# Linear attention and a squared-ReLU layer on one core: whole-group q loads, more dummy matmuls, a 384/128 last tile, and another instruction order

## The chip, the cores and the metric

The kernel runs on one core of one Trainium2 chip. A core has five engines that each run their own list of instructions in order: TensorE (PE in the profile, with its weight loads as PEld), VectorE (DVE), ScalarE (ACT), GpSimd (POOL) and SyncE (SP). Here POOL and SP mostly issue DMA transfers. The metric is the device time of one execution in microseconds (us).

## The reference

Inputs are q, k, v of shape (8 batches, 8 heads, 576 tokens, 64), a feature matrix w_phi (64 x 128), and the weights w_in (512 x 2048) and w_out (2048 x 512) of a two-layer network.

```
phi(x):  proj = x @ w_phi
         proj = proj - max(|proj|)            # per token and head
         return concat(exp(proj), exp(-proj)) # 256 features
kv  = sum over tokens of phi(k)^T v           # per batch and head
z   = sum over tokens of phi(k)
x   = (phi(q) @ kv) / (phi(q) @ z + 1e-6)     # heads side by side: 4608 x 512
out = relu(x @ w_in)^2 @ w_out                # 4608 x 512, float32
```

## The kernel before

**Tiling.** Each batch has 576 tokens: 512 "main" ones and 64 at the end. A main tile holds 128 partitions with four tokens each. The output layer takes tokens in chunks of 512: chunks 0 to 7 are the main tokens of batches 0 to 7, chunk 8 gathers the last 64 tokens of all eight batches (buffer `xS`).

**Attention of one batch** (`attention(b)`). k, q and v are loaded by POOL with a cast to bf16 into `xk`, `xq`, `xv`, two buffers each, so batch b+2 reuses the buffer of batch b. k and q must then be transposed so that the head dimension lies on partitions (`kT`, `qT`). For batches 0 and 1 PE does it with an identity (L307) and ACT or DVE copies the result; from batch 2 on SP issues a DMA transpose of the whole tile (L317). PE multiplies by `wphi2` (L333 and L482 give token-major projections whose absolute maximum DVE takes, L388 and L489; L524 gives feature-major projections of q), ACT takes the exponentials into `kp`, `kn`, `qp`, `qn` (L394, L539). PE sums `kv` (L449, L454), and later multiplies q features with it (L603, once with `qp`, once with `qn`, DVE scaling in between, L615). DVE divides (L625, L629) into `xo`, and from batch 1 on SP issues another DMA transpose from `xo` into `xT` (L663).

**The two layers.** `ffn_in` (L744, for chunk 0 in smaller pieces at L755, L769, L783) fills one bank of PSUM with 512 columns; ACT or DVE takes the ReLU into `hr` (L721, L723) and DVE squares it into `h2` (L730). `ffn_out` (L837) sums 16 matmuls of 512 columns per output tile, ACT or DVE copies the bank into `ot` (three buffers in a ring; the copy is line L190 on DVE and L192 on ACT), and SP issues the store (L855, and L852 for chunk 8). The very last output tile goes through `last_out` (L801): two halves of 256 columns in two banks, ACT copying the first and DVE the second into `otl`, then four stores (L824), two from SP and two from ACT.

**Order.** Nothing is left to a scheduler. Each step is an `Op` with an engine and a place in the list of its creation (`seq`). `ORDER` lists all of them in the order in which they are issued, and every engine executes its own part of that list in sequence. `BASES` gives each PSUM tile its bank, `STATES` chooses between ACT and DVE for copies and ReLUs that either can do (`plan.either`), and `GATES` names, for loads from batch 2 on, an earlier step after which the load may go out. `FILL` names steps before which dummy matmuls of a zero tile `warm` are put on PE (L910), as (bank, count). The waits themselves follow from the data.

```
for op in plan.arrange():
    if op.seq in FILL:
        now[0] = filler
        bank, n = FILL[op.seq]
        for _ in range(n):
            pin(nc.tensor.matmul(out=psum[:, bank, :P], lhsT=warm, rhs=warm, start=True, stop=True))
    now[0] = op
    op.fn()
```

**Layout of q.** `load_q` splits the four tokens of a partition into two pairs (`jj`) and puts, for each pair, the eight heads side by side: block t = 8 * jj + h of 128 columns. From batch 2 on it does so in `PIECES`, one pair of heads per transfer: eight transfers per batch, each with runs of 128 numbers.

Of the kernel before, what the change touches and what calls it, by code (L numbers as in the profile page):

```python
# [107 lines left out]
def kernel(  # L108
# [150 lines left out]
    def load_q(b, jjs=(0, 1), single=True, release=False, prs=((0, 4),)):  # L259

        x = xq[b % 2]
        for jj in jjs:
            for a, z in prs:
                def fn(jj=jj, a=a, z=z):
                    pin(nc.gpsimd.dma_start(  # L265
                        out=x[:, jj * 1024 + a * 256 : jj * 1024 + z * 256].rearrange("p (h x) -> p h x", x=128),
                        in_=q[b][2 * a : 2 * z, 0:512, :].rearrange("h (p j) d -> p h (j d)", j=4)[:, :, jj * 128 : jj * 128 + 128]))
                add("POOL", (0.72, 0), fn, w=([("xq", b % 2, jj)] if z == 4 else []) + [("xq", b % 2, jj, y) for y in range(a, min(z, 3))],
                     dma=(work(b, LD["main"] / 8 * (z - a)), SW_IN, "ld", late(b)), release=release, what="xq")
        if single:  # L270
            load(q, xq, b, "xq", prs=(), release=release)
# [23 lines left out]
    def attention(b):  # L295
# [173 lines left out]
        def q_ts(c):  # L469
            if c == 4:  # L470
                return [16, 17]
            return [8 * (c // 2) + h for h in range(8)] if first else [8 * (c // 2) + 4 * (c % 2) + i for i in range(4)]
# [36 lines left out]
        def q_ops(c):  # L509
# [3 lines left out]
            def fn():  # L513
                o = ps2(pf)
                for u in range(2):
# [5 lines left out]
                    else:  # L521
                        r = slice(64 * u, 64 * u + 64)
                        rhs = qTb[r, ts[0] : ts[-1] + 1, :]
# [269 lines left out]
    def last_out(c, tt, part):  # L793
# [3 lines left out]
        gs = opb[c, tt]  # L797
        def mm(half):
            def fn():
                for mc in range(4 * part, 4 * part + 4):  # L800
                    pin(nc.tensor.matmul(out=ps1(gs[half])[:, :256], lhsT=h2[c % 2][mc // 4][:, mc % 4, tt * P : (tt + 1) * P],  # L801
                                         rhs=wout[mc // 4][:, mc % 4, half * 256 : half * 256 + 256],
                                         start=(mc == 0), stop=(mc == MC - 1)))
            return fn
        for half in range(2):
            add("PE", pe_cost(4, 0.109), mm(half),
# [4 lines left out]
        for half in range(2):  # L811
            def fn(half=half):
                o, i_ = otl[:, half * 256 : half * 256 + 256], ps1(gs[half])[:, :256]
# [4 lines left out]
            add("DVE" if half else "ACT", (dve_cost if half else act_cost)(256), fn, r=[gs[half]],  # L818
                w=[("otl", half)], closes=gs[half], what="oth")
        for half in range(2):  # L820
            for u, (name, e) in enumerate((("SP", nc.sync), ("ACT", nc.scalar))):
                def fn(half=half, u=u, e=e):
                    b = 2 * tt + u
                    pin(e.dma_start(out=out[b * S + 512 : b * S + 576, half * 256 : half * 256 + 256],  # L824
                                    in_=otl[u * 64 : u * 64 + 64, half * 256 : half * 256 + 256]))
                add(name, (0.5, 2.4), fn, r=[("otl", half)], what="stl")
# [237 lines left out]
```

## Time and profile before

| | us |
|---|---|
| median of three runs | 357.9 (357.79 to 360.02) |
| the profiled execution | 359.46 |
| its span, first to last instruction | 357.7 |
| TensorE busy | 343.7 (96%) |
| VectorE busy | 276.4 (77%) |
| ScalarE busy | 227.9 (64%) |
| GpSimd busy (issue of loads) | 113.1 (32%) |

"Busy" is the time in which an engine had an instruction in work; on TensorE it includes the dummy matmuls. The profile also has a table of the span in 40 slices of 8.9 us, groups of instructions by source line, the chain of waits, and lists in order of time in which "[2.02 <-DMA out]" means that the engine sat idle for 2.02 us before the instruction and what ended it. SPq and POOLq are issues of transfers; "landed" is the time at which a transfer's last byte was reported.

### The profile page before, as it was taken

How to read it: one execution, taken by the hardware profiler on the slowest of the kernel's cores; microseconds unless marked ns; L12 is line 12 of the kernel's file. 1: busy time of each engine (PE TensorE's matmuls, PEld its weight loads, DVE VectorE, ACT ScalarE, POOL GpSimd, SP SyncE). 2: the span in 40 equal slices, each digit the busy share in tenths (PEclk: the TensorE clock that was granted, in tenths of full speed). 3: DMA queues.
4: the chain of work that ended last, by engine and by line, in shares of the span. 5: the costliest groups of instructions: out<-in, count | busy, mean ns of one | idle time of the engine just before them, and what ended most of it. 6: DMA issues, size and time to landing. Idle time of an engine off the chain costs nothing.

```text
span 357.7 us, 8393 instructions
## 1 busy us (share of the span) xinstructions
PE 343.7 (96%) x3344; PEld 194.8 (54%) x3374; DVE 276.4 (77%) x523; ACT 227.9 (64%) x429; POOL 113.1 (32%) x168
## 2 busy tenths in 40 slices
PE   6999999799999999999999999999999999999995
PEld 4789667444566455446545545455546554444443
DVE  3899899969979998799868899998849762673621
ACT  3999898549886876776689766786684700312211
POOL 8723764395706940594806000003000000000000
PEclk9999999989999999999999999999999999999999
DMA  9999999999988999796999574405400312000124
GB/s 99 187 205 199 95 165 135 162 182 171 115 130 175 141 131 177 162 158 85 127 183 148 98 98 76 139 9 58 95 3 31 95 39 88 2 0 0 73 77 117
DMA packets 102647, 39.61 MB, mean 111 GB/s; under 512 B 77264, under 2 KB 98128, under 8 KB 102608
## 3 DMA queue, kind: packets, MB, share of 16 engines
q0 software_dynamic: 51760, 18.36, 47.7%
q1 hardware_dynamic: 50608, 20.55, 27.2%
q8 instruction: 26, 0.43, 0.5%
q10 hardware_dynamic: 240, 0.16, 0.2%
q14 instruction: 13, 0.11, 0.1%
HBM read 36.77 MB, written 9.44 MB: 129 GB/s over the span
## 4 chain that ended last, share of the span: by engine, by line
PE 73%; ACT 8%; DVE 7%; POOL 4%; DMA 3%; issue 3%; SPq 0%; POOLq 0%; ACTq 0%; DVEq 0%
PE psum L837 29%; PE psum L744 24%; PE psum L603 5%; PE psum L333 4%; DVE va L421 3%; PE psum L449 2%; PE psum L524 2%; DMA xv<-in_v_dram 2%; POOL xk L245 2%; ACT qp L539 2%; ACT qn L539 1%; DMA out_dram<-ot 1%; DVE mq L489 1%; DVE h L730 1%; PE psum L769 1%
## 5 line engine op out<-in xcount | busy, mean ns | idle before, releaser
L837 PE MATMUL psum<-wout,h 128*128 128x512 bf16 x530 | 130.2, 381 | 2.3 <-issue 1.0
L744 PE MATMUL psum<-xT,win 128*128 128x512 bf16 x448 | 104.7, 380 | 0.5 <-ACT hr L721 0.3
L721 ACT ACTIVATE hr<-psum 128x512 bf16<-128x512 f32 x95 | 55.4, 599 | 61.8 <-PE psum L744 45.7
L837 PEld LDWEIGHTS <-h 128*128 128x128 bf16 x560 | 50.8, 98 | 54.3 <-issue 1.7
L744 PEld LDWEIGHTS <-win 128*128 128x128 bf16 x512 | 47.4, 98 | 53.8 <-issue 2.7
L730 DVE TENSOR_TENSOR h<-hr 128x512 bf16<-128x512 bf16 x144 | 56.0, 417 | 9.6 <-ACT hr L721 8.9
L539 ACT ACTIVATE qp<-psum 128x1024 bf16<-128x1024 f32 (+1 forms) x40 | 37.4, 936 | 18.1 <-PE psum L524 14.9
L489 DVE TENSOR_REDUCE mq<-psum 128x8 f32<-128x1024 f32 (+1 forms) x40 | 43.8, 1111 | 6.0 <-PE psum L333 5.3
L265 POOL DMA_DIRECT2D xq<-in_q_dram x52 | 39.1, 778 | 23.1 <-ACT va L413 17.4
L723 DVE TENSOR_SCALAR hr<-psum 128x512 bf16<-128x512 f32 x49 | 33.3, 685 | 14.8 <-PE psum L744 14.1
L388 DVE TENSOR_REDUCE mk<-psum 128x8 f32<-128x1024 f32 (+1 forms) x35 | 38.3, 1109 | 3.9 <-PE psum L333 3.5
L394 ACT ACTIVATE kp<-psum 128x1024 bf16<-128x1024 f32 (+1 forms) x35 | 32.8, 937 | 12.1 <-DVE mk L388 12.0
L245 POOL DMA_DIRECT2D xv<-in_v_dram x27 | 20.5, 767 | 59.6 <-DVE kv L190 49.1
L539 ACT ACTIVATE qn<-psum 128x1024 bf16<-128x1024 f32 (+1 forms) x40 | 37.4, 936 | 1.6 <-PE psum L603 1.6
L394 ACT ACTIVATE kn<-psum 128x1024 bf16<-128x1024 f32 (+1 forms) x35 | 32.7, 938 | 0.0
L615 DVE TENSOR_TENSOR psum<-psum,en 128x520 f32<-128x520 f32 (+1 forms) x39 | 26.9, 701 | 6.9 <-PE psum L603 4.8
L421 DVE TENSOR_TENSOR va<-xv,va 64x256 bf16<-64x256 bf16 (+2 forms) x66 | 29.8, 473 | 2.6 <-ACT va L413 1.6
L629 DVE TENSOR_TENSOR xo<-psum,rden 128x512 bf16<-128x512 f32 (+1 forms) x39 | 26.8, 687 | 0.9
L190 DVE COPY ot<-psum 128x512 f32<-128x512 f32 x19 | 12.9, 681 | 18.4 <-PE psum L837 15.2
L245 POOL DMA_DIRECT2D xk<-in_k_dram x28 | 21.2, 766 | 10.7 <-ACT qp L539 6.6
L449 PE MATMUL psum<-va,kp 128*128 128x65 bf16 x256 | 19.8, 193 | 0.3 <-ACT hr L721 0.3
L192 ACT ACTIVATE ot<-psum 128x512 f32<-128x512 f32 x16 | 9.6, 598 | 15.8 <-PE psum L837 13.8
(81 smaller groups left out, 408.6 us busy)
## 6 DMA issues: line engine op xcount, KB each, us to landing
out_dram<-ot SPq DMA_DIRECT2D x32, 256.0 KB, 2.8
xk<-in_k_dram POOLq DMA_DIRECT2D x26, 128.0 KB, 4.1
xq<-in_q_dram POOLq DMA_DIRECT2D x48, 64.0 KB, 4.3
xv<-in_v_dram POOLq DMA_DIRECT2D x24, 128.0 KB, 4.0
win<-in_moe_w_in_dram POOLq DMA_DIRECT2D x4, 512.0 KB, 12.6
wout<-in_moe_w_out_dram POOLq DMA_DIRECT2D x4, 512.0 KB, 8.5
xq<-in_q_dram POOLq DMA_DIRECT2D x4, 256.0 KB, 8.3
out_dram<-ot SPq DMA_DIRECT2D x6, 128.0 KB, 2.3
```

What stands on the lines that cost most here:

```text
L245: pin(nc.gpsimd.dma_start(out=x[:, a * 512 : z * 512].rearrange("p (h x) -> p h x", x=4 * D), in_=src[b][2 * a : 2 * z, 0:512, :].rearrang ...
L265: pin(nc.gpsimd.dma_start(out=x[:, jj * 1024 + a * 256 : jj * 1024 + z * 256].rearrange("p (h x) -> p h x", x=128), in_=q[b][2 * a : 2 * z ...
L388: pin(nc.vector.tensor_reduce(out=mk_view(g), in_=ps2(pj)[:, :, : n * Fd].rearrange("p e (i f) -> p e i f", f=Fd), axis=AX.X, op=ALU.max, ...
L394: pin(nc.scalar.activation(out=dst[slot][:, :, :n, :].rearrange("p e i f -> p e (i f)"), in_=ps2(pj)[:, :, : n * Fd], func=ACT.Exp, scale= ...
L421: pin(nc.vector.tensor_tensor(out=t[:, :, :D].rearrange("p m (x c) -> p m x c", c=2), in0=x.rearrange("p (m x c) -> p m x c", m=n, c=2), i ...
L489: pin(nc.vector.tensor_reduce(out=mqb[:, c, :, :n], in_=ps2(pj)[:, :, : n * Fd].rearrange("p e (i f) -> p e i f", f=Fd), axis=AX.X, op=ALU ...
L539: pin(nc.scalar.activation(out=o, in_=i_, func=ACT.Exp, scale=sgn))
L721: pin(nc.scalar.activation(out=hr[sl], in_=ps1(g), func=ACT.Relu))
L723: pin(nc.vector.tensor_scalar(out=hr[sl], in0=ps1(g), scalar1=0.0, scalar2=None, op0=ALU.max))
L730: pin(nc.vector.tensor_tensor(out=dst, in0=i_, in1=i_, op=ALU.mult))
L744: pin(nc.tensor.matmul(out=o, lhsT=win[mc // 4][:, kc, mc % 4 * P : (mc % 4 + 1) * P], rhs=x, start=(kc == 0), stop=(kc == KC - 1)))
L837: pin(nc.tensor.matmul(out=ps1(g), lhsT=h2[c % 2][mc // 4][:, mc % 4, tt * P : (tt + 1) * P], rhs=wout[mc // 4][:, mc % 4, :], start=(mc = ...
```

## The change

From batch 2 on q is loaded by pairs of heads with all four tokens of a partition together: four transfers per batch, each with runs of 256 numbers. The blocks of `qT` then lie as t = 2 * h + jj, so the lists of blocks change (`q_ts`), and the matmul that reads four of them takes every other one. The last output tile is cut at column 384. The lists `ORDER`, `BASES`, `STATES`, `GATES` and `FILL` are replaced; `FILL` goes from 114 to 142 dummy matmuls in all. The number of steps goes from 1762 to 1738, by the 24 loads that are no longer there.

```diff
     def load_q(b, jjs=(0, 1), single=True, release=False, prs=((0, 4),)):
 
         x = xq[b % 2]
+        if b >= 2:
+            for y in range(4):
+                def fn(y=y):
+                    pin(nc.gpsimd.dma_start(
+                        out=x[:, y * 512 : y * 512 + 512].rearrange("p (h x) -> p h x", x=4 * D),
+                        in_=q[b][2 * y : 2 * y + 2, 0:512, :].rearrange("h (p j) d -> p h (j d)", j=4)))
+                add("POOL", (0.72, 0), fn, w=[("xq", b % 2, jj, y) if y < 3 else ("xq", b % 2, jj) for jj in range(2)],
+                    dma=(work(b, LD["main"] / 4), SW_IN, "ld", late(b)), release=release, what="xqr")
+            jjs = ()
...
         def q_ts(c):
...
+            if b >= 2:
+                return [2 * (4 * (c % 2) + i) + c // 2 for i in range(4)]
...
-                        rhs = qTb[r, ts[0] : ts[-1] + 1, :]
+                        rhs = qTb[r, ts[0] : ts[-1] + 1 : ts[1] - ts[0], :]
...
+        C0, CW = (0, 384), (384, 128)
...
-                    pin(nc.tensor.matmul(out=ps1(gs[half])[:, :256], lhsT=h2[c % 2][mc // 4][:, mc % 4, tt * P : (tt + 1) * P],
-                                         rhs=wout[mc // 4][:, mc % 4, half * 256 : half * 256 + 256],
+                    pin(nc.tensor.matmul(out=ps1(gs[half])[:, : CW[half]], lhsT=h2[c % 2][mc // 4][:, mc % 4, tt * P : (tt + 1) * P],
+                                         rhs=wout[mc // 4][:, mc % 4, C0[half] : C0[half] + CW[half]],
...
-                o, i_ = otl[:, half * 256 : half * 256 + 256], ps1(gs[half])[:, :256]
+                o, i_ = otl[:, C0[half] : C0[half] + CW[half]], ps1(gs[half])[:, : CW[half]]
...
-                    pin(e.dma_start(out=out[b * S + 512 : b * S + 576, half * 256 : half * 256 + 256],
-                                    in_=otl[u * 64 : u * 64 + 64, half * 256 : half * 256 + 256]))
+                    pin(e.dma_start(out=out[b * S + 512 : b * S + 576, C0[half] : C0[half] + CW[half]],
+                                    in_=otl[u * 64 : u * 64 + 64, C0[half] : C0[half] + CW[half]]))
...
 FILL = {
-    41: (0, 8), 43: (0, 7), 63: (0, 2), 65: (0, 12), 85: (0, 3), 87: (0, 7), 76: (0, 9), 52: (0, 25), 119: (5, 21),
-    116: (5, 13), 122: (6, 4), 152: (0, 2), 175: (2, 1),
+    41: (0, 26), 43: (0, 6), 63: (0, 3), 65: (0, 13), 50: (0, 3), 87: (0, 5), 76: (0, 16), 106: (0, 42), 119: (0,
+    13), 122: (6, 5), 130: (0, 5), 137: (0, 2), 152: (4, 1), 329: (0, 2),
 }
```

The order of SP's first issues, before and after: before, q transposes of batch 2, first `xT` transposes of batch 1, k transposes of batch 2, first output store, three more `xT`; after, q transposes, first output store, first `xT`, k transposes, three more `xT`. In the last output tile, the new order has all 16 matmuls of the 384 columns ahead of the 16 of the 128 columns.

More of the change, by code (lines that the diff above doesn't have):

```diff
@@ L805, in last_out @@
         for half in range(2):
-            add("PE", pe_cost(4, 0.109), mm(half),
+            add("PE", pe_cost(4, CW[half] / 2400 + 0.0025), mm(half),
                 r=[("wout", part)] + [("h2", c % 2, 4 * part + i, tt) for i in range(4)],
@@ L817, in fn @@
                     pin(nc.scalar.activation(out=o, in_=i_, func=ACT.Copy))
-            add("DVE" if half else "ACT", (dve_cost if half else act_cost)(256), fn, r=[gs[half]],
+            add("DVE" if half else "ACT", (dve_cost if half else act_cost)(CW[half]), fn, r=[gs[half]],
                 w=[("otl", half)], closes=gs[half], what="oth")
@@ L823, in fn @@
                     b = 2 * tt + u
-                    pin(e.dma_start(out=out[b * S + 512 : b * S + 576, half * 256 : half * 256 + 256],
-                                    in_=otl[u * 64 : u * 64 + 64, half * 256 : half * 256 + 256]))
-                add(name, (0.5, 2.4), fn, r=[("otl", half)], what="stl")
+                    pin(e.dma_start(out=out[b * S + 512 : b * S + 576, C0[half] : C0[half] + CW[half]],
+                                    in_=otl[u * 64 : u * 64 + 64, C0[half] : C0[half] + CW[half]]))
+                add(name, (0.5, 2.2 if half else 2.6), fn, r=[("otl", half)], what="stl")
     def ffn_out(c, tt, part):
@@ L916 @@
 ORDER = [
[87 rows of a table removed]
[86 rows of a table added]
 ]
 BASES = (
-    '7761415542723630336040762373224245600440250445235741254104664375400002024062660033262307233235250266'
-    '4210166220620402664446451573423525514340262643217640042026206400006147154560444505456424061040020042'
-    '2040620033727223776635277455266263223020246004662020353225413045415746040066276650262604020200005554'
-    '2457575443564647640246355224222002402204277176732747766567475405116701754005742477666040262536241366'
-    '25367'
+    '7767715543436622132220767165712404222560646000777103064544450671264242660642446665746753616720006422'
+    '6035462222624260066612617130540005441154060225340064622220424422450561507104611146770464056672022042'
+    '4646026076611077776614577644440604776220206002206404557570466754312356522424247572040002242446247663'
+    '7765645767517617022061671444066420244402207333063071777016326726636542302746113074127362232563074213'
+    '37523'
 )
 STATES = (
-    '1000000101000001011110111000001010000101000010000001010110001010000010011000001010001010110101000001'
-    '1000001000100010000010110100100010000011111000101000001000000101100110001010001000101011100110000111'
-    '1110110100101101001111100101001'
+    '0000010111011001001000110000100000000000000000101001011000001010100010000010011101001100100001100000'
+    '1100010010010000100100110001010010001100100000000000010101000000110001000000000100110000000100011001'
+    '0010001010010111011010111100000'
 )
 GATES = {
[12 rows of a table removed]
[11 rows of a table added]
 }
 FILL = {
-    41: (0, 8), 43: (0, 7), 63: (0, 2), 65: (0, 12), 85: (0, 3), 87: (0, 7), 76: (0, 9), 52: (0, 25), 119: (5, 21),
-    116: (5, 13), 122: (6, 4), 152: (0, 2), 175: (2, 1),
+    41: (0, 26), 43: (0, 6), 63: (0, 3), 65: (0, 13), 50: (0, 3), 87: (0, 5), 76: (0, 16), 106: (0, 42), 119: (0,
+    13), 122: (6, 5), 130: (0, 5), 137: (0, 2), 152: (4, 1), 329: (0, 2),
 }
```

196 rows, old and new, of tables (GATES, ORDER) are left out of this document.

## The prediction

> **What bounds the kernel now.** I read the page's busy shares and slices first, then the busy time by stretches, then the order of instructions where a stretch falls short.
>
> ```profile
> PE 343.7 (96%) x3344; PEld 194.8 (54%) x3374; DVE 276.4 (77%) x523; ACT 227.9 (64%) x429; POOL 113.1 (32%) x168
> ...
> PE   6999999799999999999999999999999999999995
> ...
> DVE  3899899969979998799868899998849762673621
> ...
> DMA  9999999999988999796999574405400312000124
> ```
>
> TensorE is nearly full from the second slice on, with one dip (the eighth slice) and an end at half. A busy PE is partly dummy matmuls and waiting, so I added up start-to-start times of matmuls: 216 ns for 512 columns, 109 for 256, 56 for 128. Useful work is about 320 us of the 357.7. The rest lies in four places: the first 30 us, the dip, a few us of switches between kinds of matmul, and 4 us of tail.
>
> ```profile
> 0.00:10.00 10.00, 6.45 (x63) 5.46 (x64) 3.36 (x11) 4.36 (x7) 8.90 (x17) 1.00 0.95 107
> ...
> 60.00:70.00 10.00, 9.61 (x115) 5.56 (x115) 9.60 (x19) 5.98 (x13) 3.20 (x6) 1.00 1.19 167
> 70.00:80.00 10.00, 8.24 (x68) 4.12 (x69) 6.58 (x9) 5.48 (x8) 10.00 (x16) 0.83 1.39 177
> 80.00:90.00 10.00, 9.65 (x57) 4.35 (x56) 9.71 (x20) 9.84 (x21) 6.00 (x9) 1.00 1.36 164
> ```
>
> (Columns: stretch, its length, busy us of PE, PEld, DVE, ACT, POOL, then granted clock, DMA share, GB/s.) From 70 to 80 us PE lacks 1.76 us, and a granted clock of 0.83 costs 1.7 us more. DVE and ACT idle there too, so nobody gains from it. Who waits is in the time order:
>
> ```profile
> 64.08 3.00 SPq L317 DMA_TRANSPOSE kT<-xk  x1
> ...
> 67.14 0.58 SPq L855 DMA_DIRECT2D out_dram<-ot  x1
> ...
> 67.77 3.87 SPq L663 DMA_TRANSPOSE xT<-xo  x3
> ...
> 69.98 0.60 ACT L192 ACTIVATE ot<-psum 128x512 f32<-128x512 f32 x1 [2.02 <-DMA out_dram<-ot]
> 70.47 1.02 ACT L539 ACTIVATE qn<-psum 128x1024 bf16<-128x1024 f32 x1
> 71.54 0.57 PE L603 MATMUL psum<-kv,qp 128*128 128x65 bf16 x8 [1.88 <-ACT qn L539]
> ...
> 75.97 3.62 PE L744 MATMUL psum<-xT,win 128*128 128x512 bf16 x16
> ```
>
> The first output store (67.14) stood in SP's queue behind the k transposes of batch 2, though its tile was copied at 54.62. It landed at 69.95; the fourth output copy reuses that buffer, so ACT sat 2.02 us, its exponential came late, and PE idled 1.88 us and then ran cold. There is a second limit right behind: chunk 1's first matmul (75.97) needs the three xT transposes that follow in the same queue, and the last of them, issued at 70.43, took 5.3 us to land (75.75). Both hang on SP's order. The k transposes could not start before 64.08 because a k load issued at 55.16 took 8.8 us, beside the q transposes (issued 54.70, landed after 9.5 us).
>
> **Term 1: the dip, -3.2 us (bounds -3.6 to 0).** In the new order SP issues the first store right after batch 2's q transposes and before the first xT and the k transposes. It then has 5.7 us of PE work before the copy that reuses its buffer, against 2.7 before; store and landing need 0.6 + 2.8. That removes ACT's wait. What is late next is the xT chain. Batch 2's q now comes in four loads, not eight, with the last released by the second exponential of batch 1's first q tile (47.16 to 48.18 here) instead of several earlier gates. It would issue near 48.2 and, at the 3.4 us that the k load at 51.83 took, land near 52; the q transposes then start there instead of at 54.70. The five k loads follow it on POOL at 0.7 us each, all issued by 52.4, before the q transposes crowd the DMA engines: landed by 58, not 64.0. SP then does store (0.6), first xT (1.2; its input is ready at 60.5), k transposes (3.0) until 64.7, and the other three xT by 68.9, bounded by the last xo at 67.48. Landing 4.0 to 5.3 us gives 72 to 73. PE without the wait arrives, counting its matmuls from 69.66 on, at 72.5. So 75.97 becomes 72.5 to 73: -3.2. If the loads come no earlier, nothing is gained.
>
> **Term 2: start, -0.6 us (bounds -1.2 to +1.6).** Dummies grow from 114 to 142, 26 instead of 8 ahead of the first transpose.
>
> ```profile
> 0.99 1.04 PE L910 MATMUL psum<-warm 128*128 128x128 bf16 x8 [0.99 <-DVE warm L226]
> ...
> 4.59 0.59 PE L307 MATMUL psum<-ident,xk 128*128 128x128 bf16 x4 [2.56 <-POOL ident L862]
> ...
> 7.02 1.49 PE L910 MATMUL psum<-warm 128*128 128x128 bf16 x12
> ```
>
> Until 10.1 us every 128-column matmul starts 107 ns after the last, afterwards 56: PE is at half speed although the slices show a 9. 26 dummies at 107 ns end at 3.8 us, still before the first load lands (4.47), so they delay nothing. Real work at half speed between 4.59 and 10.13 is 16 transposes (51 ns lost each) and 16 tiled matmuls (0.2 us per eight): 1.2 us, and ACT waits 2.1 us for it in pieces before it becomes continuous at 11.1. I take half. [...] On the other side, 28 dummies at 56 ns standing in front of ready work would cost 1.6. Work ahead of chunk 1 is otherwise the same on PE, and ACT and DVE together, moved by under 1 us.
>
> **Term 3: switches, -0.7 us (bounds -1 to 0).** Going from full-array matmuls to the two-row-half kind (L333, L524) costs a median 96 ns, and 120 back. The new order has 95 such crossings, not 102: 7 x 0.11.
>
> **Term 4: tail, -0.3 us (bounds -0.4 to +0.1).**
>
> ```profile
> 351.34 2.35 PE L801 MATMUL psum<-wout,h 128*128 128x256 bf16 x20
> ...
> 353.73 0.38 ACT L817 ACTIVATE otl<-psum 128x256 f32<-128x256 f32 x1 [2.45 <-PE psum L801]
> 353.79 1.20 SPq L824 DMA_DIRECT2D out_dram<-otl  x2
> ```
>
> Now the last store goes out at 354.44, 0.75 us after the last matmul, since the half that ends last meets an occupied SP. With 384 first and 128 last, sixteen 128-column matmuls (0.9 us) cover the 384 copy (0.49, between 0.38 and 0.60 for 256 and 512 on ACT) and its stores; after them come a 128-column DVE copy (0.29 on the line through 0.42 and 0.69) and an issue: about 0.4. PE time is the same: 16 x 162 + 16 x 56 ns against 32 x 109; the 162 is halfway between 109 and 216.
>
> **Costed at nothing.** The q loads:
>
> ```profile
> q0 software_dynamic: 51760, 18.36, 47.7%
> ...
> xq<-in_q_dram POOLq DMA_DIRECT2D x48, 64.0 KB, 4.3
> ```
>
> 48 issues become 24 (-18 us of POOL, which is no bound), and 12288 packets of 256 B at 44.5 ns become 6144 of 512 B at 69.1: 7.6 us less per DMA engine over six batches. PE has other work beside them; with that cover gone it would be term 1. A bigger packet could also hold a transpose back longer, at most 25 ns each. The features' matmul now reads every other block of 128 columns; L744 reads its input in that way at 216 ns, the full rate. Some 15 evacuations move from DVE to ACT (0.69 to 0.60 each), which relieves the fuller engine.
>
> **Term 5: new waits, +1.0 us (bounds 0 to 3.8).** Counted in PE work, two later stores stand only 1.7 and 1.9 us ahead of the copy that reuses their buffer (the tightest before: 2.6). Behind such a copy stand all evacuations of its engine. Of three tight ones before, one idled PE 1.9 us, two (DVE waits of 0.7 and 2.4 us) cost PE nothing. Two at a third of 1.9 is 1.3; I take 1.0, as 1.2 to 1.5 us of the store's time is left uncovered, against 0.7.
>
> **Sum:** -3.2 - 0.6 - 0.7 - 0.3 + 1.0 = -3.8. The profiled execution took 359.46 us (span 357.7 and 1.8 around it), so 355.7 in its terms. The three runs' median is 357.9; the dip's order is the same in every run, so I subtract there too: **354.1 us**.
>
> **Rivals.** (a) The gain is swallowed: DVE, 9.6 to 9.7 busy of 10 between 80 and 100 us, becomes the bound, or the xT landing still ends last. For it: DVE has hardly a gap there. Against: it lost 3 us of its own in the dip. Half of term 1 goes: 356 to 357.5. (b) A reused output buffer stalls PE again with a cold window: 1.9 + 1.7 us, once or twice: 357 to 360.5. (c) Slower: the fourth q load is the last before SP's first transposes, has only 5.0 us of PE work ahead of them (before: 7.2), and SP issues in order. Loads beside weights landed after 13 to 15 us early on, q loads at 43 to 46 us after 7.5 to 8.3. Lands it at 57, nothing is gained; at 63 (14 us), batch 2's q arrives at 72.5 instead of the needed 66.5: 6 us idle, 1.7 of half clock, less terms 2 to 4: 364. It decides from 57 us on. For it: the gate is late and two weight loads stand before it. Against: they land by about 40 to 47 us here. (d) q loads do lighten the DMA but the order gives nothing: 357 to 358.
>
> **Chances.** Forecast (351.8 to 356) 0.50, (a) 0.16, (b) 0.12, (c) 0.14, (d) 0.08. Faster by over 1% (below 354.3; about what can be told from no change) is the better half of the forecast and a bit: 0.35; within 1% 0.48; slower 0.17, with the top of (b). The range for 8 in 10 reaches to (b): 351.8 to 360.5.
>
> **What would show it.** Right: no PE gap over 0.5 us between 60 and 80 us; the first store issued within 10 us of its copy; chunk 1's first matmul near 72 to 73 us; 56 ns matmuls from about 7 us; last store within 0.5 us of the last matmul. Wrong: q transposes later than 55 us, ACT or DVE waiting on a store with PE behind it, or DVE solid and PE gapped from 75 to 115 us.

## The result, and the profile after

| | before | after |
|---|---|---|
| median of nine runs, us | 358.5 (357.64 to 360.7) | 354.13 (353.35 to 356.43) |
| ratio of after to before | | 0.988, 95% interval 0.985 to 0.991 |
| the profiled execution, us | 359.46 | 353.35 |
| its span, us | 357.7 | 351.3 |

The change saves 4.3 us (interval 3.3 to 5.4); 354.1 was forecast. The two profiled executions differ by 6.1 us, since before's lay 1.0 above its median and after's is the fastest of its nine. Differences read from these two traces therefore add up to some 1.8 us too much.

The page of after, busy shares, slices of 8.8 us and the queue of the casting loads:

```profile
PE 343.6 (98%) x3402; PEld 193.1 (55%) x3402; DVE 267.2 (76%) x511; ACT 234.9 (67%) x441; POOL 96.2 (27%) x144
...
PE   8899999999999999999999999999999999999995
...
DVE  5999898999989997898868987998668532645610
...
DMA  8999999999979999999559774102310113000114
...
q0 software_dynamic: 45232, 18.36, 45.1%
```

The dip in the eighth slice is gone. POOL issues 24 loads less and is busy 17 us less (18 were worked out). The casting loads took 47.7% of 357.7 us before and 45.1% of 351.3 now: 12 us less per DMA engine between these two executions (7.6 were worked out; the rest is not explained).

The busy time by stretches of after, with the columns of the prediction's fence:

```profile
0.00:10.00 10.00, 8.28 (x120) 7.09 (x120) 5.81 (x17) 5.53 (x11) 8.82 (x17) 1.00 0.95 109
...
60.00:70.00 10.00, 10.00 (x122) 5.59 (x121) 9.73 (x18) 5.41 (x11) 4.87 (x8) 1.00 0.80 123
70.00:80.00 10.00, 9.78 (x62) 4.29 (x60) 9.40 (x17) 9.52 (x19) 8.57 (x13) 1.00 1.22 136
80.00:90.00 10.00, 10.00 (x102) 5.27 (x101) 9.88 (x22) 9.66 (x19) 5.11 (x8) 1.00 1.30 180
```

From 70 to 80 us PE was busy 8.24 us at a granted clock of 0.83; it is now busy 9.78 at 1.00. DVE does 9.40 us of work there, where it did 6.58. Who came earlier is in the time order of after (SP's issues, ACT's fourth output copy, chunk 1's first matmul):

```profile
50.13 5.81 SPq L326 DMA_TRANSPOSE qT<-xq  x1
...
55.99 0.58 SPq L867 DMA_DIRECT2D out_dram<-ot  x1
...
57.96 1.20 SPq L674 DMA_TRANSPOSE xT<-xo  x1
...
59.40 3.88 SPq L326 DMA_TRANSPOSE kT<-xk  x1
...
63.33 3.87 SPq L674 DMA_TRANSPOSE xT<-xo  x3
...
64.02 0.60 ACT L192 ACTIVATE ot<-psum 128x512 f32<-128x512 f32 x1
...
69.74 2.61 PE L755 MATMUL psum<-xT,win 128*128 128x512 bf16 x10
```

The store goes out at 55.99 instead of 67.14, the copy at 64.02 has no wait, the k transposes start at 59.40 instead of 64.08, and chunk 1 starts at 69.74 instead of 75.97. From there to the last matmul both kernels need the same time: 277.45 us before, 277.54 after. So in these two traces the whole gain lies ahead of chunk 1, but for the tail:

```profile
343.84 3.66 PE L813 MATMUL psum<-wout,h 128*128 128x384 bf16 x32
...
346.64 0.49 ACT L829 ACTIVATE otl<-psum 128x384 f32<-128x384 f32 x1 [2.00 <-PE psum L813]
347.16 1.43 SPq L836 DMA_DIRECT2D out_dram<-otl  x2
347.16 1.26 ACTq L836 DMA_DIRECT2D out_dram<-otl  x2
347.61 0.29 DVE L827 COPY otl<-psum 128x128 f32<-128x128 f32 x1 [8.72 <-PE psum L813]
```

The last matmul starts at 347.28 (until 347.50), the last store is issued at 347.93, and the span ends 4.01 us after that start, against 4.27 before.

### The profile page after: what moved, and what is told of

Read it like the earlier page. It is cut to its first block, busy times and chain, and to the rows that moved or that the text cites. A ratio compares the mean times of both kernels' runs of the same rounds, so it can differ in the third digit from the quotient of the medians.

```text
span 351.3 us, 8451 instructions
## 1 busy us (share of the span) xinstructions
PE 343.6 (98%) x3402; PEld 193.1 (55%) x3402; DVE 267.2 (76%) x511; ACT 234.9 (67%) x441; POOL 96.2 (27%) x144
## 3 DMA queue, kind: packets, MB, share of 16 engines
q0 software_dynamic: 45232, 18.36, 45.1%
## 4 chain that ended last, share of the span: by engine, by line
PE 76%; ACT 12%; DVE 7%; issue 2%; DMA 2%; DVEq 0%; ACTq 0%; POOLq 0%
PE psum L849 31%; PE psum L755 24%; PE psum L614 5%; PE psum L342 4%; PE psum L458 3%; ACT hr L732 2%; PE psum L535 2%; PE psum L794 2%; ACT kp L403 2%; DVE mk L397 2%; DVE h L741 1%; ACT kp L385 1%; DMA xT<-xo 1%; ACT kn L403 1%; ACT kn L385 1%
## 5 line engine op out<-in xcount | busy, mean ns | idle before, releaser
L849 PE MATMUL psum<-wout,h 128*128 128x512 bf16 x560 | 132.6, 379 | 0.1
L755 PE MATMUL psum<-xT,win 128*128 128x512 bf16 x448 | 105.6, 379 | 0.5 <-DVE hr L734 0.2
L732 ACT ACTIVATE hr<-psum 128x512 bf16<-128x512 f32 x101 | 58.3, 596 | 39.0 <-PE psum L755 20.9
L755 PEld LDWEIGHTS <-win 128*128 128x128 bf16 x512 | 47.2, 98 | 53.5 <-issue 3.4
L734 DVE TENSOR_SCALAR hr<-psum 128x512 bf16<-128x512 f32 x43 | 29.3, 686 | 26.8 <-PE psum L755 26.0
L192 ACT ACTIVATE ot<-psum 128x512 f32<-128x512 f32 x25 | 14.7, 596 | 31.2 <-PE psum L849 29.4
L265 POOL DMA_DIRECT2D xq<-in_q_dram x24 | 17.7, 753 | 9.7 <-ACT qp L550 5.0
L458 PE MATMUL psum<-va,kn 128*128 128x65 bf16 x256 | 19.6, 193 | 0.0
```

Source lines behind the costliest of these rows:

```text
L458: pin(nc.tensor.matmul(out=o[:, sg, hi, :], lhsT=(kp, kn)[sg][kgroup[pr]][:, j % 2, 2 * hi + j // 2, :], rhs=va[s2][sg][:, 8 * pr + 4 * hi ...
L732: pin(nc.scalar.activation(out=hr[sl], in_=ps1(g), func=ACT.Relu))
L734: pin(nc.vector.tensor_scalar(out=hr[sl], in0=ps1(g), scalar1=0.0, scalar2=None, op0=ALU.max))
L755: pin(nc.tensor.matmul(out=o, lhsT=win[mc // 4][:, kc, mc % 4 * P : (mc % 4 + 1) * P], rhs=x, start=(kc == 0), stop=(kc == KC - 1)))
L849: pin(nc.tensor.matmul(out=ps1(g), lhsT=h2[c % 2][mc // 4][:, mc % 4, tt * P : (tt + 1) * P], rhs=wout[mc // 4][:, mc % 4, :], start=(mc = ...
```

## The experiments

Each kernel was timed against before on the same chip; the numbers below are medians and ratios of such runs. One execution of before can lie anywhere from 356.3 to 361.2 us, so a trace tells here which wait is possible and the medians tell what it is worth. In the tables a gain in us is one less the ratio, times 358.5.

### The old order with single parts of the change

**Store alone.** SP's list ahead of chunk 1, changed in the kernel before:

```diff
   qT transposes of batch 2
+  first output store
   first xT transposes of batch 1
   kT transposes of batch 2
-  first output store
   three more xT transposes
```

> The kernel before with one move in SP's order: the first output store stands right after the q transposes of batch 2 (as in the changed kernel), not after the k transposes. Theory 'store': ACT's 2.0 us wait and PE's 1.9 us gap near 70 us go, and with them most of the dip: -3 us. Theory 'xT chain': the wait goes as well, but chunk 1's first matmul still waits for the last xT transpose, whose place in SP's queue moves up by the store's 0.6 us alone: 75.97 becomes about 75.3, total -0.3 to -0.8 us.

**Gate alone.** The first q load of batch 2 may go out without waiting for an earlier step (a ReLU of chunk 0):

```diff
 GATES = {
-    383: 339,
```

> The kernel before with one gate taken away: the first-pair load of batch 2's q that POOL holds from 32.4 to 37.8 us until a ReLU is done (with two weight and v loads queued behind it) goes out as soon as its buffer is free. SP's order is unchanged. Theory 'xT chain' (what ends last is the loads of batch 2, since SP issues in order): POOL's 5.5 us gap goes, q transposes start near 50 and not 54.7, k transposes near 60, the store behind them lands near 66 and the last xT near 71, so both waits vanish: -3 us. Theory 'store': nothing that matters moves, ACT still waits for a store that stands behind the k transposes: 0 to -1 us.

**Both.**

> Both edits, store moved and gate taken away. Theory 'xT chain': as the gate alone, -3 to -3.6 us. Theory 'store': as the store alone. If each removes one of two waits that both have to go: -3.4 us here and under 1 us in each of the two others.

**Dummies alone.**

```diff
 FILL = {
-    41: (0, 8),
+    41: (0, 26),
```

> The kernel before with 26 instead of 8 dummy matmuls ahead of the first transpose, nothing else. Theory 'start passes through': the clock is full from about 4 us on and not from 10, the start gains 0.6 to 1.9 us (the first matmul of the first layer at 24.5 to 25.8 and not 26.4 us) and the whole kernel as much. Rival 'swallowed by the dip': the first layer starts earlier, but chunk 1's first matmul still waits for the transposes near 75 us, so the total gains under 0.4 us.

**Whole-group q loads alone** (`load_q`, `q_ts` and the strided read of the new kernel, the lists of the old one with 24 loads taken out):

> The kernel before with whole-group q loads alone (24 issues for 48; each keeps the place of the later of its two pieces and the gates; tail 256/256, 8 first dummies, old order). Queue theory: four issues less per batch, at 0.7 us each, bring batch 2's k loads forward as taking the gate away did (-2.4 us), and later transposes are less crowded, as the eight-piece kernel in the new order says (+3.1 us): -2 to -3.5 us against before. Cover theory (the forecast's 'costed at nothing'): in the old order the loads lie beside other work, and the dip is set by the gate: -0.7 to +0.5 us.

**Four together** (whole-group q loads, gate, store, 26 dummies, in the old order):

> The kernel before with four edits and nothing else of the new order: whole-group q loads, gate of the first q load of batch 2 taken away, first output store right behind the q transposes of batch 2, 26 first dummies. If these four are the change, -4 to -5 us against before, as much as the full change (-4.3). If gate and q loads use the same slack on POOL's queue, and the rest of the new order brings something of its own, -2.5 to -3.3 us.

| against before | median us | ratio (interval) | gain, us |
|---|---|---|---|
| store | 358.05 | 0.9986 (0.9955 to 1.0018) | 0.5, unclear |
| gate | 356.19 | 0.9933 (0.9906 to 0.9960) | 2.4 |
| store and gate | 355.62 | 0.9921 (0.9892 to 0.9949) | 2.8 |
| 26 dummies | 358.54 | 0.9996 (0.9965 to 1.0027) | 0.1, none |
| whole-group q loads | 356.46 | 0.9936 (0.9913 to 0.9959) | 2.3 |
| all four | 356.07 | 0.9933 (0.9909 to 0.9957) | 2.4 |
| the whole change | 354.13 | 0.9880 (0.9850 to 0.9909) | 4.3 |

Store alone does next to nothing by the median, although it does what it is for: in its trace ACT's wait of 2.02 us is gone. (That trace is the shortest of its twelve executions and has no PE wait ahead of chunk 1, so it can't show what holds up the others.) The gate alone brings 2.4. It changes nothing in SP's list, but lets k in earlier, and with it all that stands behind the k transposes on SP: the first store goes out at 64.76 instead of 67.14, and the three xT follow it. In its trace ACT still waits 1.15 us for that store, and PE 1.02. So what costs most is the late k load, which reaches PE through the store and through xT; the store's own place adds 0.4 to 0.5. That xT can bind by itself is seen in the trace of both edits, the longest of its twelve:

```profile
74.38 0.61 PE L744 MATMUL psum<-xT,win 128*128 128x512 bf16 x2 [1.50 <-DMA xT<-xo]
```

The gate acts through POOL's queue. Its issues in before, with what ended the idle time ahead of them:

```profile
37.84 2.12 POOL L265 DMA_DIRECT2D xq<-in_q_dram  x3 [5.47 <-ACT kT L192]
...
42.60 0.97 POOL L245 DMA_DIRECT2D xv<-in_v_dram  x1
...
51.83 0.71 POOL L245 DMA_DIRECT2D xk<-in_k_dram  x1 [3.31 <-DMA xv<-in_v_dram]
```

and the same k load without the gate (first line) and, in a second kernel's trace, with the gate but with whole-group q loads:

```profile
49.09 0.71 POOL L245 DMA_DIRECT2D xk<-in_k_dram  x1 [3.29 <-DMA xv<-in_v_dram]
```

```profile
49.22 0.72 POOL L245 DMA_DIRECT2D xk<-in_k_dram  x1 [3.44 <-ACT va L416]
```

POOL sat 5.47 us behind one gated load while batch 1's v load (42.60) stood behind it. In all seven traces of the old order the first k load goes out 0.53 us after that v load has landed. Its own gate, an exponential of batch 1's q, had ended at 47.26 in before; why it waits for the v load is not shown. Without the gate it goes out 2.7 us earlier, and with three q issues less ahead of the v load 2.6 us earlier. Each edit alone is worth 2.3 to 2.4.

All four together bring no more than one, and SP's queue shows why. The k transposes stand behind the first xT transpose there. In before they were issued 2.4 us after it had left SP, as soon as the last k load had landed (64.00). Without the gate, with whole groups and with all four edits they follow it after 0.23 us, so nothing is left to gain at this place, although with all four the first k load goes out at 47.53 already. SP with all four:

```profile
60.47 1.21 SPq L674 DMA_TRANSPOSE xT<-xo  x1
61.92 3.90 SPq L326 DMA_TRANSPOSE kT<-xk  x1
```

The queue theory of the whole-group kernel fits (2 to 3.5 us expected, 2.3 measured), and of the four-edit kernel the case in which gate and q loads use the same slack (2.5 to 3.3 expected, 2.4 measured, interval 1.5 to 3.3). Some 1.9 us of the full gain (4.3 less 2.4, about 1.4 to either side) come from none of the four edits.

The dummies show how an earlier start can be swallowed. In the traced execution the early work starts 1.9 us earlier than in before, yet chunk 1 starts at 77.52, 1.55 us later. Its ACT and PE:

```profile
71.56 0.60 ACT L192 ACTIVATE ot<-psum 128x512 f32<-128x512 f32 x1 [5.45 <-DMA out_dram<-ot]
```

```profile
73.12 0.60 PE L603 MATMUL psum<-kv,qp 128*128 128x65 bf16 x8 [5.32 <-ACT qn L539]
```

The store waited for here was issued at 66.34, behind k transposes that could not start before 63.55, nearly as late as in before (64.08). PE arrived earlier and waited longer.

### The new order with single parts undone

Each is the kernel after with one part put back: 8 instead of 26 dummies ahead of the first transpose; the first store behind the k transposes again; the last tile cut at 256; q in eight pieces from batch 2 on, at the places and gates of the four groups:

```diff
 FILL = {
-    41: (0, 26),
+    41: (0, 8),
```

> The changed kernel with 8 instead of 26 dummy matmuls ahead of the first transpose. If the start's gain of about 1.9 us (first matmul of the first layer at 24.4 and not 26.4 us) comes from the clock: +0.6 to +1.9 us, and that matmul back at 25 to 26.3. If it comes from the order (the first copy on VectorE, v ahead of q): within 0.4 us.

```diff
   qT transposes of batch 2
-  first output store
   first xT transposes of batch 1
   kT transposes of batch 2
+  first output store
   three more xT transposes
```

> The changed kernel with its first output store back behind the k transposes in SP's order, just ahead of the second xT. Theory 'store': ACT waits again before the fourth output copy and PE stalls: +2 to +3.5 us. Theory 'xT chain': the k transposes end at 63.3 here, the store lands by 66.5, ACT reaches the copy at 64.0 and waits 2 us for it, yet PE has other work until about 66 us: 0 to +1.5 us.

```diff
-        C0, CW = (0, 384), (384, 128)
+        C0, CW = (0, 256), (256, 256)
```

> The changed kernel with the last output tile cut at 256 and not at 384, in the changed order (first all of the first half, then the second). By the prediction's numbers the split alone is worth 0.42 - 0.29 = 0.13 us of VectorE's copy; the rest of the tail's 0.3 us comes from the order: +0.1 us, not to be told from none.

```diff
     def load_q(b, jjs=(0, 1), single=True, release=False, prs=((0, 4),)):
-        if b >= 2:
+        if False:
...
         def q_ts(c):
-            if b >= 2:
+            if False:
```

> The changed kernel with q from batch 2 on loaded by eight transfers again, each of the four replaced by its two at the same place and with the same gate (and the blocks of qT as before). By the prediction the lighter loads are worth nothing as long as PE has other work: within 0.4 us. Rival: POOL issues four more loads per batch, 2.9 us, ahead of the k loads of batch 2, the k and xT transposes start later and the dip comes back in part: +1 to +3 us.

| put back | median us | ratio to before (interval) | lost against after, us |
|---|---|---|---|
| 256/256 tail | 354.55 | 0.9878 (0.9852 to 0.9903) | none seen |
| first store | 355.60 | 0.9900 (0.9875 to 0.9925) | 0.7, unclear |
| 8 dummies | 356.14 | 0.9920 (0.9897 to 0.9943) | 1.4 (about 1.4 to either side) |
| eight q pieces | 357.53 | 0.9966 (0.9945 to 0.9988) | 3.1 (about 1.3 to either side) |

Putting the store back costs what the 'xT chain' theory allows (0 to 1.5) and less than the 'store' theory's 2 to 3.5. The dummies' 1.4 fits a gain by the clock (0.6 to 1.9), and the q pieces' 3.1 is far from the "within 0.4 us" that was expected by the prediction.

The traces cut the time at two places that every kernel has: the first matmul of chunk 0's first layer (L769, after L780) and chunk 1's first matmul (L744, after L755).

| profiled execution | chunk 0 starts | chunk 0 to chunk 1 | chunk 1 to last matmul | last matmul to end |
|---|---|---|---|---|
| before | 26.36 | 49.61 | 277.45 | 4.27 |
| old order, store | 26.03 | 46.13 | 277.57 | 4.27 |
| old order, gate | 26.12 | 47.20 | 276.94 | 4.24 |
| old order, both | 25.80 | 48.58 | 277.98 | 4.23 |
| old order, dummies | 24.49 | 53.03 | 277.17 | 4.28 |
| old order, q loads | 25.81 | 47.26 | 277.16 | 4.24 |
| old order, four edits | 26.33 | 46.12 | 277.74 | 4.24 |
| after | 24.44 | 45.30 | 277.54 | 4.01 |
| after, 8 dummies | 25.51 | 45.29 | 279.00 | 4.01 |
| after, store back | 26.19 | 45.45 | 277.98 | 3.99 |
| after, tail back | 26.15 | 45.29 | 277.15 | 4.31 |
| after, eight q pieces | 26.34 | 45.29 | 280.73 | 4.00 |

The third column is the main finding. In the old order this stretch takes 46.1 us where PE waits for nothing in it (store, four edits), and more by its waits elsewhere, up to 53.0 us; in the new order it takes 45.3 to 45.5, whichever part is undone. What stands behind this, measured from chunk 0's start:

| us after chunk 0's start | k transposes issued | first store landed | last xT landed | longest PE wait before chunk 1 |
|---|---|---|---|---|
| before | 37.73 | 43.60 | 49.39 | 1.88 |
| old order, gate | 35.57 | 42.73 | 46.65 | 1.02 |
| old order, q loads | 35.59 | 42.79 | 47.38 | 1.08 |
| old order, store | 36.14 | 37.43 | 47.11 | 0.15 |
| old order, four edits | 35.59 | 32.68 | 46.37 | 0.15 |
| after | 34.96 | 34.62 | 45.98 | 0.14 |
| after, store back | 34.95 | 40.92 | 44.39 | 0.16 |
| after, tail back | 35.14 | 37.64 | 44.99 | 0.16 |

Three things differ. The k transposes and xT come a little earlier in the new order; batch 1's v load, on which the k loads hung, is issued there at 30.64 us, ahead of batch 2's q. There is slack for the store: with the store put back ACT waits 1.56 us for it and PE does not wait, where 1.15 us of ACT cost PE 1.02 in the old order without the gate:

```profile
67.19 0.60 ACT L192 ACTIVATE ot<-psum 128x512 f32<-128x512 f32 x1 [1.56 <-DMA out_dram<-ot]
```

And PE itself needs 0.8 us less for the same matmuls (46.1 to 45.3; one dummy of 639 is gone): those that read `wphi` border on others 32 times in this stretch in the old order and 26 times in the new. Which of the many moved steps gives the slack was not isolated.

The fourth column of the table of stages tells where the eight pieces cost: not at the dip, as the rival in the expectation had it, but near 104 and 141 us. SP's transposes and store near 130 us in the kernel with eight pieces, and the copy and matmul that wait for the store:

```profile
127.06 8.74 SPq L326 DMA_TRANSPOSE qT<-xq  x2
...
137.23 1.44 SPq L867 DMA_DIRECT2D out_dram<-ot  x1
...
140.94 0.69 DVE L190 COPY ot<-psum 128x512 f32<-128x512 f32 x1 [2.05 <-DMA out_dram<-ot]
...
141.69 2.75 PE L849 MATMUL psum<-wout,h 128*128 128x512 bf16 x12 [1.75 <-DVE ot L190]
```

The same steps with whole groups (the kernel with only the tail put back):

```profile
125.53 5.98 SPq L326 DMA_TRANSPOSE qT<-xq  x2
...
132.92 0.52 SPq L867 DMA_DIRECT2D out_dram<-ot  x1
...
137.35 0.68 DVE L190 COPY ot<-psum 128x512 f32<-128x512 f32 x1
```

With eight pieces POOL issued its last load ahead of this place at 129.40, in the midst of the transposes, and with whole groups at 122.28, before them. The first q transposes then took 8.89 us to land instead of 4.55, the store went out at 137.23 instead of 132.92, and DVE waited 2.05 us for its buffer. This step costs 1.9 us between the two traces, and a smaller one near 104 us 1.1 more. That other executions lose about as much is told by the median (3.1), that it is lost at this place only by this one. Eight pieces mean both more issues (48 against 24) and smaller packets (256 B against 512 B), and no run separates the two.

The 8-dummy kernel shows the same kind of wait at another tile, one of the two pairs that the prediction's term 5 had picked out (only 1.7 us of PE work between a store and the copy that reuses its buffer). Store, copy and matmul:

```profile
212.29 0.33 SPq L867 DMA_DIRECT2D out_dram<-ot  x1
...
216.79 0.60 ACT L192 ACTIVATE ot<-psum 128x512 f32<-128x512 f32 x1 [2.63 <-DMA out_dram<-ot]
217.44 1.89 PE L849 MATMUL psum<-wout,h 128*128 128x512 bf16 x8 [1.57 <-ACT ot L192]
```

The store took 4.4 us to land; in after's trace the same store took 2.1 us, and nobody waited. This accounts for 1.6 us in this execution that have nothing to do with dummies.

### Four output buffers: an experiment that missed

If reused output buffers are what costs, a fourth one should take the cost away. `ring("ot", 3)` became 4 and the slot `oslot[0] % 3` became `% 4`, in the kernel with eight pieces and in after.

> The kernel after with eight-piece q loads (which measured -1.2 us against before, some 3.1 us more than the kernel after) and four output buffers instead of three. Store theory: the added issues hold the q transposes of a later batch (8.9 us instead of 4.6 near 127 us), behind them on SP stands an output store, and the copy that reuses its buffer makes PE wait (1.7 us near 140 us); a fourth buffer ends that: -3 to -4 us against before. Load theory: what is late is q, k or xT itself, and buffers for the output do nothing: -0.7 to -1.7 us.

> The kernel after with four output buffers instead of three, nothing else. Store theory: single executions of it and its neighbours lose 0.8 to 1.6 us at a reused output buffer (near 105 us, near 213 us), so -4.8 to -5.8 us against before, the fastest of all. If those waits are rare: -4.0 to -4.6 us, as the kernel after.

Measured: 363.84 us (ratio 1.0142, 1.0099 to 1.0184) with eight pieces and 359.21 (1.0006, 0.9981 to 1.0031) with whole groups, so against the same kernels with three buffers they lost 6.3 and 4.5 us where a gain or nothing was expected. The cause was found afterwards in the lists. Buffers are dealt out as the steps are created, while `ORDER` issues copies and stores in another sequence, made for three buffers. With four, tile 9 shares a buffer with tile 5, whose store stands directly ahead of 9's copy (no PE work between them, against 3.3 to 4.1 us for the stores ahead of the copies of tiles 8, 9 and 11 with three). Two other tiles (27 and 30) are written over 23 and 26 before those are stored, so these two kernels leave out part of the output. They can't tell whether more buffers would help; that needs slots dealt out by the order of issue and was not tried. What they do show is the price of one such wait. Store, copy and matmul in after with four buffers:

```profile
137.14 0.57 SPq L867 DMA_DIRECT2D out_dram<-ot  x1
...
140.05 0.69 DVE L190 COPY ot<-psum 128x512 f32<-128x512 f32 x1 [2.57 <-DMA out_dram<-ot]
...
140.79 4.31 PE L849 MATMUL psum<-wout,h 128*128 128x512 bf16 x12 [2.26 <-DVE ot L190]
```

```profile
140.00:150.00 10.00, 9.21 (x60) 3.86 (x60) 7.99 (x10) 5.80 (x8) 6.45 (x10) 0.83 0.75 128
```

PE idles 2.26 us, then runs at half clock (12 matmuls in 4.31 us, where the eight-piece kernel needs 2.75), and the granted clock of the stretch is 0.83. Compared instruction by instruction with the tail-back kernel, 4.0 us are lost at this one place. The mean granted clock is 0.995 or less in 11 of this kernel's 12 executions and 0.998 or more in all nine of after, so the traced one is probably not alone with its half clock.

## Why the prediction was right, and where it was not

**The total** came out at 354.13 for a forecast of 354.1, and "faster by over 1%" (0.35) happened, narrowly: 1.2%, interval 0.9 to 1.5. That the two times agree so closely is luck: before's median is 358.5 and not 357.9, and the gain 4.3 and not 3.8. It is luck in its parts too. With q in eight pieces the new order gains only 1.2 us (0.4 to 2.0), so 3.1 of the 4.3 rest on an edit that the sum put at nothing. The terms one by one:

**Term 1, the dip (-3.2, bounds -3.6 to 0): right in size for the traced execution, half wrong in cause.** Between the two traces the stretch from chunk 0 to chunk 1 shrank by 4.3 us, beyond the bound: 3.5 are the wait (1.88) and the half clock behind it (a granted clock of 0.50 from 71.60 to 75.01 us), as forecast, and 0.8 belong to term 3. But "the dip's order is the same in every run, so I subtract there too" holds for the order and not for its price. Of the 74 executions of before timed beside the experiments, 22 show a mean granted clock of 0.995 or less, as the traced one does; their median is 360.3 us, that of the other 52 (0.997 or more) 358.4. So some three executions in ten probably have the half clock (where it lies in them is not recorded), and its 1.6 us should not have been taken off a median. If before's excess of 1.0 over its median lies in this stretch, the typical gain there is 3.3 (an estimate). The step "that removes ACT's wait" was right, and the store alone was worth 0.5 (-0.6 to 1.6). "Both hang on SP's order" is half right: both stand in SP's queue, but what holds that queue up is the k load, which hangs on POOL's (2.4 by the gate, 2.3 by the q loads). "If the loads come no earlier, nothing is gained" was not tested in the new order, where the k transposes were issued 35 us after chunk 0's start in every trace.

**Term 2, the start (-0.6, bounds -1.2 to +1.6): right as a mean, wrong as a picture.** It is not half a gain but a whole one in some executions. The first rows of PE in after:

```profile
0.99 2.95 PE L922 MATMUL psum<-warm 128*128 128x128 bf16 x26 [0.99 <-DVE warm L226]
4.37 0.40 PE L316 MATMUL psum<-ident,xk 128*128 128x128 bf16 x4 [0.43 <-DMA xk<-in_k_dram]
```

and in the tail-back kernel, which is the same up to here:

```profile
0.99 2.95 PE L922 MATMUL psum<-warm 128*128 128x128 bf16 x26 [0.99 <-DVE warm L226]
4.41 0.61 PE L316 MATMUL psum<-ident,xk 128*128 128x128 bf16 x4 [0.46 <-DMA xk<-in_k_dram]
```

Four transposes in 0.40 us at full rate, or 0.61 at half rate. With 26 dummies the rate doubled before 5 us in three of eight profiled executions (after, the old order with dummies, four buffers) and at 9.8 to 10.3 us in five; with 8 dummies it never came before 8.0 us in six. The early ones start chunk 0 at 24.4 to 25.1 us, the late ones at 26.2 to 26.4. Three in eight times the 1.7 us between after and its tail-back twin is 0.6 (an estimate). No run shows the -0.6 as such: half of the 1.2 us was the author's estimate, and before's trace does not tell whether a longer train brings the doubling forward. What the runs showed in its place is that, behind the same first instructions, the rate doubled at 3.9 us in one execution (after) and at 9.8 in another (its tail-back twin). What decides between the two is not shown. In before's trace the rate doubled at 10.16 us, the granted clock fell to 0.50 at 71.60 and was back at 1.00 at 75.01; of the two distances, 61.44 and 3.413 us, the first is 18 times the second. By medians the dummies are worth 1.4 (0 to 2.8) in the new order and 0.1 (-1.0 to 1.3) in the old, where the dip swallowed them in the one trace.

**Term 3, switches (-0.7): right in size, ahead of chunk 1 alone.** By a count in the traces, matmuls that read `wphi` border on others 118 times in before and 108 times in after. All ten lie ahead of chunk 1, behind it both have 68. Between executions in which PE waited for nothing there the stretch from chunk 0 to chunk 1 is 0.8 us shorter (46.1 to 45.3). That the switches alone make the 0.8 was not tested.

**Term 5, new waits (+1.0):** from chunk 1 to the last matmul the two traces differ by 0.1 us, so it came to nothing in them. The waits are real: with the dummies put back one took 1.6 us, at a pair named in term 5, and after has none in its one trace. A fixed +1.0 stands for a mean over executions in which it was 0 or some 1.6.

**Term 4, the tail (-0.3):** 4.27 to 4.01 us, and back to 4.31 with the cut at 256. The medians can't see it.

**"Costed at nothing" is the step that failed.** The q loads are worth 2.3 us in the old order and 3.1 in the new. The prediction looked at the DMA engines, where other work lies beside them, and at POOL as "no bound". It did not follow what is queued behind them: in the old order three issues of 0.7 us less ahead of the v load on which batch 2's k loads wait, and in the new order eight-piece loads that run into q transposes with an output store behind them on SP. In the old order this gain and that of the gate are the same microseconds, and term 1 had named the earlier k loads; the 3.1 of the new order lie near 104 and 141 us, where no term had looked for a gain.

**The rivals.** (a) did not happen: DVE is as full as before between 80 and 90 us (9.9 of 10, before 9.7), PE is busy all of that stretch, and the gain stands. (b) did not happen in after. Its price, 1.9 + 1.7 us for one wait and the half clock behind it, was measured at 4.0 in the four-buffer kernel. (c) did not happen: the last q load of batch 2 was issued at 46.51, not 48.2, and the q transposes started at 50.13, far from the 57 us at which it decides. (d) is half right: the q loads do bring something, and more than it gave them (356.5 alone), but the order brings some 1.9 us more.

Of the marks given, the first store's issue (9.7 us after its copy), the absence of a PE gap over 0.5 us near the dip, and the last store (0.43 us after the last matmul's end) came as described. Matmuls at 56 ns came from 4.4 us on in after's trace and from 9.8 in its twin's, not from the 7 that the author had estimated. Chunk 1's first matmul came at 69.74, earlier than the 72 to 73 named, because chunk 0 began 1.9 us earlier in that execution; in the twin it came at 71.44.

## What to carry to other kernels

- A load that is no bound on its engine still has a place in a queue. Cost an edit of it by the transfers that stand behind it and by what they feed, not by the busy share of the engine that issues it: a wait of 5.5 us on one gated load held up a k load whose own gate had long been passed.
- Two edits that each move the same late transfer are not to be added: 2.4 and 2.3 us alone were 2.4 together with two edits more. Look for what stands next in the queue: here the first xT transpose. Slack at the place that waits is worth more: the reordered kernel keeps its 45.3 us, to within 0.2, when any single edit is undone.
- Where buffers are dealt out at creation and issued by a separate list, more buffers can mean less distance. Work out the distance from store to reuse before trying it.

## What was not expected of the hardware

- A k load issued just behind the first q transposes landed late. Over the fourteen traces, the 11 issued within 0.9 us after them took 6.0 to 9.6 us to land (before 8.84, the tail-back kernel 9.63), and the 70 issued up to 5 us ahead of them 2.6 to 6.5.
- A PE gap of 1.88 us was followed by half clock in before (0.50 over 3.41 us), and so were one of 2.26 with four buffers (0.83 over the stretch of 10 us) and one of 5.32 with dummies in the old order (four matmuls of `ffn_out` in 1.90 us behind it, 1.04 ahead of it). Gaps of 1.75 and 1.57 us, of the eight-piece and the 8-dummy kernel, were not (12 and 8 matmuls of 512 columns in 2.75 and 1.89 us). Where the step lies, and whether it is a matter of length or of the moment, stays open.
- In the first 10 us of before the granted clock stands at 1.00 although matmuls of 128 columns follow each other at 107 ns. In the dips, half rate is shown as 0.83 for a stretch of 10 us (in before, 0.50 over 3.41 us of it). The start is to be read from the matmuls' own intervals.
